# GELU feed-forward layer with its gradients: a smaller clear, b1 in two transfers, another bank for the first grad_out block, w2 evictions shared out, and gw1's half groups in a row at the end

## The chip, the cores and the metric

The kernel runs on one core of a Trainium2 chip. The metric is the time of one execution on the device in microseconds (us), where lower is better. Three runs of the kernel before gave a median of 285.6 us (285.5 to 286.16).

## The reference

The forward pass is a dense layer, a GELU in its tanh form and a second dense layer. The reference returns the output and the gradients of all five inputs:

```python
B, S, D, F = 1, 2048, 448, 1792        # everything in bf16
h = einsum("bsd,df->bsf", x, w1) + b1
h = gelu_tanh(h)
out = einsum("bsf,fd->bsd", h, w2) + b2
# and the vjp for grad_out:  gx, gw1, gb1, gw2, gb2
```

## The kernel before

D = 448 is three blocks of 128 and a rest of 64, so KD = 4 and the last block holds 64 rows only. The token axis is cut into 8 blocks of 256, the F axis into 7 pairs of 128-wide tiles. A step `n` is one pair in one block, 56 steps in all. The order of every instruction is written out by hand (`manual_schedule`), and each engine works through its own list in that order.

**Main loop, per step.** `M1` (L202) makes the pre-activation of two F tiles: 8 matmuls, four contraction blocks kt = 0 to 3 for each of the two tiles. The fourth block, kt = 3, uses `w1_sb[:, 3, :]`: its upper 64 partitions hold the rest of w1, its lower 64 are zero but for row 0, which holds b1. Row 0 of the fourth block of `xT_q` is one, so the bias comes in through the matmul. `M1` therefore needs the clear of that block, the load of w1's rest and the load of b1, at its fourth matmul. `M2` (L237) makes the output, `M4` (L224) grad_out times w2 transposed, `M6` (L255) gx, seven steps later. ScalarE (ACT) makes `hT` and the square `A`, then the tanh `Ct` and its square; VectorE (DVE) makes `Bt`, `A`, `Ep` and `ghT`; GpSimd (POOL) makes `Eq`. In block 0 there is no gx yet, and in its place TensorE turns w2 by transposes: `TR(c)` (L211) turns two tiles of w2 into a PSUM bank `psx`, and one copy (L214 on DVE or L216 on ACT) brings it into `w2T_sb`. There are seven such turns, before steps 0 to 6.

**Start.** GpSimd clears `warm` and the lower 64 partitions of `w1_sb[:, 3, :]` (L116). DVE builds the identity matrix `ident` in a chain of small instructions on `ramp` (L121) and `rowi` (L126). SP and ACT issue the loads: x of block 0 (`x_nat0`), w2 in four pieces, grad_out of block 0 (`g_nat0`), w1 in several column pieces (`load_w1`, rows of the first three blocks; `load_w1_last`, the rest), and b1 (L147) on ACT's queue behind the clear. b2 is loaded through GpSimd's queue (L157). TensorE turns x of block 0 (`turn_x0`, L175), runs `M1(0)`, `TR(0)`, turns grad_out of block 0 into a `psx` bank (`turn_g0`, L187), then `M1(1)`, `TR(1)`, `M2(0)`, `M4(0)`, `M1(2)`, `TR(2)` and so on. There are two `psx` banks, two `ps1`, two `ps4` and two output banks `pso0` and `pso1`; `M2` of a block accumulates in the output banks and `M2_out` (L243) empties them on DVE.

**End.** After the main loop come gw2 (L379) and gw1. For gw1 the F axis is cut into chunks of 256, 512, 512 and 512 columns. Each chunk has three full groups (L452: 16 matmuls with a 128x128 weight, evicted by ACT at L454 and stored by SP at L455) and then one half group, `half(ci)` (L432). A half group has 64 weight columns only, so the chunk's columns are split in two halves, and the two halves are computed side by side in the two column halves of the array (`tile_position=(0, h * DL)`): 32 matmuls. Each of the two results is evicted by itself and stored by itself (L443); for the last chunk ACT evicts the first half (L439) and DVE the second (L441).

Of the kernel before, what the change touches and what calls it, by code (L numbers as in the profile page):

```python
# [10 lines left out]
ALU = mybir.AluOpType  # L11
BF16 = mybir.dt.bfloat16
# [7 lines left out]
def kernel(  # L20
# [15 lines left out]
    nc = tc.nc  # L36
    P = 128
    B, S, D = x.shape
    F = w1.shape[1]
# [4 lines left out]
    KD = (D + P - 1) // P  # L44
    DL = D - (KD - 1) * P
# [5 lines left out]
    SPB = SB // P  # L51
# [13 lines left out]
    psop = ctx.enter_context(tc.tile_pool(name="psop", bufs=1, space=bass.MemoryType.PSUM))  # L65
    psxp = ctx.enter_context(tc.tile_pool(name="psxp", bufs=2, space=bass.MemoryType.PSUM))
# [20 lines left out]
    w1_sb = wts.tile([P, KD, F], BF16, name="w1_sb")  # L87
# [25 lines left out]
    ramp = wts.tile([P, P], F32, name="ramp")  # L113
    rowi = wts.tile([P, 32], F32, name="rowi")
    nc.gpsimd.memset(warm[:], 0.0)
    nc.gpsimd.memset(w1_sb[0:DL, KD - 1, :], 0.0)  # L116


    nc.vector.memset(ramp[:, 0:1], 0.0)
# [3 lines left out]
    for q in range(1, 4):  # L123
        nc.vector.tensor_scalar(out=rowi[32 * q:32 * q + 32, 0:1], in0=rowi[32 * q:32 * q + 32, 0:1],
                                scalar1=32.0 * q, scalar2=None, op0=ALU.add)
    nc.vector.tensor_scalar(out=ident[:], in0=ramp[:], scalar1=rowi[:, 0:1], scalar2=None, op0=ALU.is_equal)  # L126

    def load_w1(eng, f0, f1):
        eng.dma_start(out=w1_sb[:, 0:KD - 1, f0:f1],  # L129
                      in_=w1[0:(KD - 1) * P, f0:f1].rearrange("(k p) f -> p k f", p=P))  # L130

    def load_w1_last(eng, f0, f1):
        eng.dma_start(out=w1_sb[DL:P, KD - 1, f0:f1], in_=w1[(KD - 1) * P:D, f0:f1])
# [9 lines left out]
    nc.sync.dma_start(out=x_nat0[:], in_=x2[0:SB, :].rearrange("(j p) d -> p j d", p=P))  # L143
    load_w1(nc.scalar, 0, 256)
    load_w1_last(nc.scalar, 0, 512)
    nc.scalar.activation(out=warm_h[:], in_=warm[:, 0:64], func=ACT.Gelu_apprx_tanh)
    nc.scalar.dma_start(out=w1_sb[0:1, KD - 1, :], in_=b1.rearrange("(o f) -> o f", o=1))  # L147
    load_w2(nc.sync, 0, 2)
    nc.sync.dma_start(out=g_nat0[:], in_=g2[0:SB, :].rearrange("(j p) d -> p j d", p=P))  # L149
    load_w1(nc.sync, 256, 512)  # L150
    load_w2(nc.sync, 2, 4)
    load_w1(nc.sync, 512, 1024)
    load_w1_last(nc.sync, 512, F)
# [16 lines left out]
    def turn_x0(dst, src):  # L170
        for j in range(SPB):
            pt = psxp.tile([P, SPB, KD, P], BF16, name="psx")
            for kt in range(KD):
                lo = DOV if kt == KD - 1 else kt * P
                nc.tensor.transpose(pt[:, 0, kt, :], src[:, j, lo:lo + P], ident[:])  # L175
            if j == 0:
                nc.vector.tensor_copy(out=dst[:, :, j * P:(j + 1) * P], in_=pt[:, 0, :, :])
            else:
                nc.scalar.copy(out=dst[:, :, j * P:(j + 1) * P], in_=pt[:, 0, :, :])  # L179
        nc.vector.memset(dst[0:1, KD - 1, :], 1.0)  # L180

    def turn_g0(dst, src):
        pt = psxp.tile([P, SPB, KD, P], BF16, name="psx")
        for j in range(SPB):
            for kt in range(KD):
                lo = DOV if kt == KD - 1 else kt * P
                nc.tensor.transpose(pt[:, j, kt, :], src[:, j, lo:lo + P], ident[:])  # L187
        nc.scalar.copy(out=dst[:].rearrange("p k (j s) -> p j k s", j=SPB), in_=pt[:])
        nc.gpsimd.memset(dst[0:DL, KD - 1, :], 0.0)
# [16 lines left out]
    def TR(c):  # L206
        pt = psxp.tile([P, 2, KD, P], BF16, name="psx")
        for t in range(2):
            for kt in range(KD):
                lo = DOV if kt == KD - 1 else kt * P  # L210
                nc.tensor.transpose(pt[:, t, kt, :], w2_sb[:, 2 * c + t, lo:lo + P], ident[:])  # L211
        dst = w2T_sb[:, :, 2 * c * P:(2 * c + 2) * P].rearrange("p k (t f) -> p t k f", t=2)
        if c < 2:
            nc.vector.tensor_copy(out=dst, in_=pt[:])  # L214
        else:
            nc.scalar.copy(out=dst, in_=pt[:])  # L216
# [123 lines left out]
    for n in range(NSTEP):  # L340
        b, c = divmod(n, NP)
# [43 lines left out]

    with ExitStack() as wctx:
        wp = wctx.enter_context(tc.tile_pool(name="wp", bufs=1))
        gw1_all = wp.tile([P, KD, F], BF16, name="gw1_all")
        gw2_all = wp.tile([P, NF, D], BF16, name="gw2_all")
        x_all = wp.tile([P, NS, D], BF16, name="x_all")  # L390
        gsum = wp.tile([P, D], F32, name="gsum")
        gb2_w = wp.tile([P, D], BF16, name="gb2_w")
        gb1_all = wp.tile([P, F], BF16, name="gb1_all")
        gb1_row = wp.tile([1, F], BF16, name="gb1_row")
        out3_v = out_3.rearrange("(o f) -> o f", o=1)
        out4_v = out_4.rearrange("(ft p) d -> p ft d", p=P)

        chunks = [(0, 256), (256, 512), (768, 512), (1280, 512)]
        ghn = []
        for (f0, fw) in chunks:  # L400
            t = wp.tile([P, NS, fw], BF16, name=f"gh_nat{f0}")
            for k in range(fw // P):
                nc.sync.dma_start_transpose(out=t[:, :, k * P:(k + 1) * P], in_=ghT_dram[f0 + k * P:f0 + (k + 1) * P, :])
            ghn.append(t)
        nc.gpsimd.dma_start(out=x_all[:], in_=x2.rearrange("(st p) d -> p st d", p=P))

        nc.vector.tensor_reduce(out=gsum[:], in_=g_all[:].rearrange("p s d -> p d s"), axis=mybir.AxisListType.X, op=ALU.add)
        nc.gpsimd.partition_all_reduce(gb2_w[:], gsum[:], channels=P, reduce_op=bass_isa.ReduceOp.add)
        nc.gpsimd.dma_start(out=out_5.rearrange("(o d) -> o d", o=1), in_=gb2_w[0:1, :])

        for ft in range(NF):
            ps = early[ft] if ft < 2 else gw2_mm(ft)
            nc.scalar.copy(out=gw2_all[:, ft, :], in_=ps[:, 0:D])
            if ft in (4, 9, NF - 1):
                lo = {4: 0, 9: 5, NF - 1: 10}[ft]
                nc.sync.dma_start(out=out4_v[:, lo:ft + 1, :], in_=gw2_all[:, lo:ft + 1, :])

        for ci, (f0, fw) in enumerate(chunks):
            gacc = wp.tile([P, 512], F32, name="gacc", bufs=2)
            nc.vector.tensor_reduce(out=gacc[:, 0:fw], in_=ghn[ci][:].rearrange("p s f -> p f s"),  # L420
                                    axis=mybir.AxisListType.X, op=ALU.add)
            nc.gpsimd.partition_all_reduce(gb1_all[:, f0:f0 + fw], gacc[:, 0:fw], channels=P, reduce_op=bass_isa.ReduceOp.add)
        nc.gpsimd.tensor_scalar(out=gb1_row[:], in0=gb1_all[0:1, :], scalar1=0.5, scalar2=None, op0=ALU.mult)
        nc.gpsimd.dma_start(out=out3_v[0:1, :], in_=gb1_row[:])

        def half(ci):
            f0, fw = chunks[ci]
            hw = fw // 2
            ps = psxp.tile([P, 512], F32, name="psx")
            for s_ in range(NS):  # L430
                for h in range(2):
                    nc.tensor.matmul(ps[h * DL:(h + 1) * DL, 0:hw], lhsT=x_all[:, s_, (KD - 1) * P:D],  # L432
                                     rhs=ghn[ci][:, s_, h * hw:(h + 1) * hw],
                                     start=(s_ == 0), stop=(s_ == NS - 1), tile_position=(0, h * DL), skip_group_check=True)
            for h in range(2):
                src = ps[h * DL:(h + 1) * DL, 0:hw]
                dst = gw1_all[h * DL:(h + 1) * DL, KD - 1, f0 + h * hw:f0 + (h + 1) * hw]
                if h == 0 or ci + 1 < len(chunks):
                    nc.scalar.mul(out=dst, in_=src, mul=0.5)  # L439
                else:  # L440
                    nc.vector.tensor_scalar(out=dst, in0=src, scalar1=0.5, scalar2=None, op0=ALU.mult)  # L441
                eng = nc.scalar if h == 0 and ci + 1 == len(chunks) else nc.sync
                eng.dma_start(out=out_2[(KD - 1) * P:D, f0 + h * hw:f0 + (h + 1) * hw], in_=dst)  # L443

        i = 0
        for ci, (f0, fw) in enumerate(chunks):
            for kt in range(KD - 1):
                pool, name = (ps1p, "ps1") if i % 2 == 0 else (ps4p, "ps4")
                i += 1
                ps = pool.tile([P, 512], F32, name=name)  # L450
                for s_ in range(NS):
                    nc.tensor.matmul(ps[:, 0:fw], lhsT=x_all[:, s_, kt * P:(kt + 1) * P], rhs=ghn[ci][:, s_, :],  # L452
                                     start=(s_ == 0), stop=(s_ == NS - 1))
                nc.scalar.mul(out=gw1_all[:, kt, f0:f0 + fw], in_=ps[:, 0:fw], mul=0.5)  # L454
            nc.sync.dma_start(out=out_2[0:(KD - 1) * P, f0:f0 + fw].rearrange("(k p) f -> p k f", p=P),  # L455
                              in_=gw1_all[:, 0:KD - 1, f0:f0 + fw])
            half(ci)


# [28 lines left out]
```

## Time and profile before

| | |
|---|---|
| median of three runs | 285.6 us |
| the profiled execution | 285.71 us |
| its span, first to last instruction | 283.9 us |
| TensorE (PE) busy | 277.2 us, 98% |
| DVE, ACT, POOL busy | 78%, 55%, 33% |
| granted TensorE clock | 1.0 |

The profile comes from one execution. Busy time of TensorE is modelled at the end of each matmul, so two neighbouring matmuls overlap in the rows: the distance from start to start is what a matmul costs in a row of them. A row of the timeline names the start, the length, the engine, the line, the operation with its shapes, and in brackets how long the engine had been idle and what released it. A queue's name ends in q (SPq, ACTq). PEld is the loading of weights, which overlaps the matmuls.

### The profile page before, as it was taken

The page shows a single profiled execution, that of the slowest core. Times are in us where ns is not written, and L with a number is a line of the kernel's source. Part 1 is how long each engine was busy: PE and PEld are TensorE (multiplying, and loading weights), DVE is VectorE, ACT ScalarE, POOL GpSimd, SP SyncE. Part 2 cuts the span into 40 slices and gives each one's busy share as a digit, 9 for nine tenths or more (in the row PEclk, how much of TensorE's full clock was granted, in tenths as well). Part 3 has the DMA queues.
Part 4 walks back from the last instruction along what each step waited for, and adds up shares of the span by engine and source line. Part 5 has one row for each costly group of instructions (what it writes and reads, how often), then busy time and mean ns, then how long its engine had stood idle before and what let it go on. Part 6 is the DMA issues. An engine that isn't in the chain of part 4 may idle for free.

```text
span 283.9 us, 5012 instructions
## 1 busy us (share of the span) xinstructions
PE 277.2 (98%) x1969; PEld 182.7 (64%) x1969; DVE 221.1 (78%) x263; ACT 155.5 (55%) x282; POOL 94.3 (33%) x88
## 2 busy tenths in 40 slices
PE   7999999999999999999999999999999999999994
PEld 3787677777777777777777777765555557554542
DVE  5688988887888897798887888875976999999000
ACT  2799777667777667777677776752121121212211
POOL 4233343334255333433334423341052004040451
PEclk9999999999999999999999999999999999999999
DMA  7999874463558957539426453184999999501101
GB/s 201 334 147 228 165 154 123 124 117 88 164 132 257 236 149 121 134 109 148 124 85 146 102 151 98 34 196 106 327 181 208 208 181 266 168 27 38 62 5 65
DMA packets 108089, 41.96 MB, mean 148 GB/s; under 512 B 81089, under 2 KB 107137, under 8 KB 108066
## 3 DMA queue, kind: packets, MB, share of 16 engines
q1 hardware_dynamic: 106528, 37.56, 59.4%
q0 software_dynamic: 976, 3.79, 4.2%
q8 instruction: 15, 0.25, 0.4%
q10 hardware_dynamic: 562, 0.30, 0.4%
q14 instruction: 8, 0.07, 0.1%
HBM read 7.46 MB, written 14.23 MB: 76 GB/s over the span
## 4 chain that ended last, share of the span: by engine, by line
PE 94%; DMA 2%; DVE 1%; SPq 1%; ACT 1%; issue 0%; DVEq 0%
PE ps L224 17%; PE ps L202 16%; PE ps L379 15%; PE pso L237 15%; PE psx L255 15%; PE ps L452 13%; DMA w_sb<-in_w_dram 2%; PE psx L432 2%; PE psx L211 1%; DVE o_blk L243 0%; DVE Bt L282 0%; ACT hT L276 0%; ACT A L272 0%; SPq L129 0%; SPq L149 0%
## 5 line engine op out<-in xcount | busy, mean ns | idle before, releaser
L296 POOL TENSOR_TENSOR Eq<-Ct,Ep 128x512 bf16<-128x512 bf16 x56 | 64.7, 1156 | 112.9 <-DVE Ep L295 110.8
L282 DVE SCALAR_TENSOR_TENSOR Bt<-A,ps 128x512 f32<-128x512 f32 x56 | 38.4, 686 | 26.3 <-ACT A L272 26.3
L202 PE MATMUL ps<-xT_q,w_sb 128*128 128x256 bf16 x448 | 58.2, 273 | 0.4 <-ACT xT_q L179 0.2
L224 PE MATMUL ps<-gT_q,w2T_sb 128*128 128x256 bf16 x448 | 58.1, 273 | 0.1
L276 ACT ACTIVATE hT<-ps 128x512 bf16<-128x512 f32 x56 | 33.3, 595 | 44.6 <-PE ps L202 44.5
L420 DVE TENSOR_REDUCE gacc<-gh_nat 128x512 f32<-128x8192 bf16 (+1 forms) x4 | 49.7, 12460 | 4.7 <-DMA gh_nat<-ghT_dram 4.7
L224 PEld LDWEIGHTS <-w2T_sb 128*128 128x128 bf16 x448 | 43.7, 98 | 14.5 <-ACT Bt L289 0.5
L237 PE MATMUL pso<-w_sb,hT 128*128 128x448 bf16 x224 | 51.7, 352 | 0.4 <-DVE o_blk L243 0.4
L255 PE MATMUL psx<-w1T_sb,ghT 128*128 128x448 bf16 x224 | 50.5, 352 | 0.0
L202 PEld LDWEIGHTS <-w_sb 128*128 128x128 bf16 x448 | 43.7, 98 | 6.2 <-issue 0.9
L379 PE MATMUL ps<-g_all,h_nat 128*128 128x448 bf16 x224 | 42.5, 352 | 0.0
L283 DVE SCALAR_TENSOR_TENSOR A<-A,ps 128x512 f32<-128x512 f32 x56 | 38.5, 687 | 1.9
L301 DVE SCALAR_TENSOR_TENSOR ghT<-Eq,ps 128x512 bf16<-128x512 bf16 x56 | 38.2, 681 | 1.4 <-POOL Eq L296 1.3
L295 DVE SCALAR_TENSOR_TENSOR Ep<-Bt,A 128x512 bf16<-128x512 f32 x56 | 38.4, 685 | 0.4
L452 PE MATMUL ps<-gh_nat,x_all 128*128 128x512 bf16 (+1 forms) x192 | 37.0, 353 | 0.0
L289 ACT ACTIVATE Bt<-Ct 128x512 f32<-128x512 bf16 x56 | 35.3, 630 | 1.8
L288 ACT ACTIVATE Ct<-Bt 128x512 bf16<-128x512 f32 x56 | 35.6, 636 | 0.0
L379 PEld LDWEIGHTS <-h_nat 128*128 128x128 bf16 x224 | 21.9, 98 | 20.5
L237 PEld LDWEIGHTS <-hT 128*128 128x128 bf16 x224 | 21.7, 98 | 19.9 <-issue 0.9
L272 ACT ACTIVATE A<-ps 128x512 f32<-128x512 f32 x56 | 33.1, 592 | 0.0
L255 PEld LDWEIGHTS <-ghT 128*128 128x128 bf16 x224 | 21.9, 98 | 12.5
L452 PEld LDWEIGHTS <-x_all 128*128 128x128 bf16 x192 | 18.5, 98 | 17.5 <-issue 0.4
(47 smaller groups left out, 119.8 us busy)
## 6 DMA issues: line engine op xcount, KB each, us to landing
ghT_dram<-ghT SPq DMA_DIRECT2D x8, 512.0 KB, 3.0
ghT_dram<-ghT SPq DMA_DIRECT2D x8, 384.0 KB, 3.1
out_dram<-o_blk SPq DMA_DIRECT2D x8, 224.0 KB, 2.0
out_dram<-gx_blk SPq DMA_DIRECT2D x8, 224.0 KB, 2.1
g_all<-in_grad_out_dram POOLq DMA_DIRECT2D x1, 1792.0 KB, 9.6
x_all<-in_x_dram POOLq DMA_DIRECT2D x1, 1792.0 KB, 10.8
out_dram<-gw_all SPq DMA_DIRECT2D x3, 384.0 KB, 2.4
out_dram<-gw_all SPq DMA_DIRECT2D x2, 560.0 KB, 4.1
```

Of the source, the lines that this page charges most:

```text
L202: nc.tensor.matmul(ps1[:, t * SB:(t + 1) * SB], lhsT=w1_sb[:, kt, f], rhs=xq[:, kt, :], start=(kt == 0), stop=(kt == KD - 1))
L224: nc.tensor.matmul(ps4[:, t * SB:(t + 1) * SB], lhsT=w2T_sb[:, kt, (2 * c + t) * P:(2 * c + t + 1) * P], rhs=gq[:, kt, :], start=(kt == 0) ...
L237: nc.tensor.matmul(pso[j][:, 0:D], lhsT=hT[:, c, o:o + P], rhs=w2_sb[:, ft, :], start=(ft == 0), stop=(ft == NF - 1))
L255: nc.tensor.matmul(psx[:, 0:D], lhsT=ghT[:, ft // 2, o:o + P], rhs=w1T_sb[:, ft, :], start=(ft == 0), stop=(ft == NF - 1))
L282: nc.vector.scalar_tensor_tensor(out=Bt[:], in0=A[:], scalar=3.0 * GELU_C, in1=ps1[:], op0=ALU.add, op1=ALU.mult)
L283: nc.vector.scalar_tensor_tensor(out=A[:], in0=A[:], scalar=GELU_C, in1=ps1[:], op0=ALU.add, op1=ALU.mult)
L295: nc.vector.scalar_tensor_tensor(out=Ep[:], in0=s["Bt"][:], scalar=1.0, in1=s["A"][:], op0=ALU.subtract, op1=ALU.mult)
L296: nc.gpsimd.tensor_tensor(out=Eq[:], in0=s["Ct"][:], in1=Ep[:], op=ALU.subtract)
L301: nc.vector.scalar_tensor_tensor(out=blkt[b]["ghT"][:, c, :], in0=s["Eq"][:], scalar=1.0, in1=s["ps4"][:], op0=ALU.add, op1=ALU.mult)
L379: nc.tensor.matmul(ps[:, 0:D], lhsT=h_nat[:, bb * NP + c, t * SPB + sj, :], rhs=g_all[:, s_, :], start=(s_ == 0), stop=(s_ == NS - 1))
L420: nc.vector.tensor_reduce(out=gacc[:, 0:fw], in_=ghn[ci][:].rearrange("p s f -> p f s"), axis=mybir.AxisListType.X, op=ALU.add)
L452: nc.tensor.matmul(ps[:, 0:fw], lhsT=x_all[:, s_, kt * P:(kt + 1) * P], rhs=ghn[ci][:, s_, :], start=(s_ == 0), stop=(s_ == NS - 1))
```

## The change

GpSimd clears 512 of the 1792 columns of w1's fourth block; DVE clears the other 1280 after the turn of x. b1 comes in two transfers: 512 columns on ACT's queue, and 1280 columns on GpSimd's queue behind DVE's clear. The load of w1's columns 256 to 512 moves from SP's queue to ACT's, in front of b1. grad_out of block 0 is turned into the bank of `pso0`. The copies of w2's turns 3 and 5 move from ACT to DVE. In the end part all full groups of gw1 come first, and the half groups follow as chunks 1, 2, 3, 0; both halves of a half group are evicted by one ACT instruction into a small tile `low`, and all their stores go to SP, but for one of chunk 0, which goes to ACT.

```diff
-    nc.gpsimd.memset(w1_sb[0:DL, KD - 1, :], 0.0)
+    nc.gpsimd.memset(w1_sb[0:DL, KD - 1, 0:512], 0.0)
...
     load_w1(nc.scalar, 0, 256)
     load_w1_last(nc.scalar, 0, 512)
+    load_w1(nc.scalar, 256, 512)
     nc.scalar.activation(out=warm_h[:], in_=warm[:, 0:64], func=ACT.Gelu_apprx_tanh)
-    nc.scalar.dma_start(out=w1_sb[0:1, KD - 1, :], in_=b1.rearrange("(o f) -> o f", o=1))
+    b1_row = b1.rearrange("(o f) -> o f", o=1)
+    nc.scalar.dma_start(out=w1_sb[0:1, KD - 1, 0:512], in_=b1_row[:, 0:512])
     load_w2(nc.sync, 0, 2)
     nc.sync.dma_start(out=g_nat0[:], in_=g2[0:SB, :].rearrange("(j p) d -> p j d", p=P))
-    load_w1(nc.sync, 256, 512)
     load_w2(nc.sync, 2, 4)
...
         nc.vector.memset(dst[0:1, KD - 1, :], 1.0)
+        nc.vector.memset(w1_sb[0:DL, KD - 1, 512:F], 0.0)
+        nc.gpsimd.dma_start(out=w1_sb[0:1, KD - 1, 512:F], in_=b1_row[:, 512:F])
 
     def turn_g0(dst, src):
-        pt = psxp.tile([P, SPB, KD, P], BF16, name="psx")
+        pt = psop.tile([P, SPB, KD, P], BF16, name="pso0")
...
-        if c < 2:
+        if c in (0, 1, 3, 5):
             nc.vector.tensor_copy(out=dst, in_=pt[:])
         else:
             nc.scalar.copy(out=dst, in_=pt[:])
...
-        gw1_all = wp.tile([P, KD, F], BF16, name="gw1_all")
+        gw1_all = wp.tile([P, KD - 1, F], BF16, name="gw1_all")
...
+            low = wp.tile([P, 256], BF16, name="low", bufs=4)
+            nc.scalar.mul(out=low[:, 0:hw], in_=ps[:, 0:hw], mul=0.5)
             for h in range(2):
-                src = ps[h * DL:(h + 1) * DL, 0:hw]
-                dst = gw1_all[h * DL:(h + 1) * DL, KD - 1, f0 + h * hw:f0 + (h + 1) * hw]
-                if h == 0 or ci + 1 < len(chunks):
-                    nc.scalar.mul(out=dst, in_=src, mul=0.5)
-                else:
-                    nc.vector.tensor_scalar(out=dst, in0=src, scalar1=0.5, scalar2=None, op0=ALU.mult)
-                eng = nc.scalar if h == 0 and ci + 1 == len(chunks) else nc.sync
-                eng.dma_start(out=out_2[(KD - 1) * P:D, f0 + h * hw:f0 + (h + 1) * hw], in_=dst)
+                eng = nc.scalar if h == 0 and ci == 0 else nc.sync
+                eng.dma_start(out=out_2[(KD - 1) * P:D, f0 + h * hw:f0 + (h + 1) * hw], in_=low[h * DL:(h + 1) * DL, 0:hw])
...
             nc.sync.dma_start(out=out_2[0:(KD - 1) * P, f0:f0 + fw].rearrange("(k p) f -> p k f", p=P),
                               in_=gw1_all[:, 0:KD - 1, f0:f0 + fw])
-            half(ci)
+        for ci in (1, 2, 3, 0):
+            half(ci)
```

## The prediction, made before the change was run

> **What bounds the kernel now.** I read the page first: the span, the busy shares and the chain of work that ended last.
>
> ```profile
> span 283.9 us, 5012 instructions
> PE 277.2 (98%) x1969; PEld 182.7 (64%) x1969; DVE 221.1 (78%) x263; ACT 155.5 (55%) x282; POOL 94.3 (33%) x88
> PE 94%; DMA 2%; DVE 1%; SPq 1%; ACT 1%; issue 0%; DVEq 0%
> ```
>
> TensorE carries the chain for 94% of the span. So only four places can pay: the start before TensorE is fed, its stalls, what it loses between matmuls, and what follows its last matmul. The chain in order of time shows the start and the end:
>
> ```profile
> 2.76 6.88 DMA w_sb<-in_w_dram
> ...
> 236.74 5.24 PE ps L452 x48
> 241.98 1.01 PE psx L432 x32
> 243.00 10.47 PE ps L452 x48
> ...
> 278.13 1.89 PE psx L432 x32
> ```
>
> The first row is the load of w2 tiles 2 and 3, issued by SP at 2.76 and landed at 9.64. Next the timeline from 0 to 13 us, engine by engine, which shows what else was late:
>
> ```profile
> 1.19 1.62 POOL L116 MEMSET w_sb<- 64x1792 bf16 x1
> 6.50 0.46 PEld L202 LDWEIGHTS <-w_sb 128*128 128x128 bf16 x5 [0.22 <-issue]
> 8.28 1.05 PE L202 MATMUL ps<-xT_q,w_sb 128*128 128x256 bf16 x8 [0.15 <-DMA w_sb<-in_w_dram]
> 9.69 0.62 PE L211 MATMUL psx<-ident,w_sb 128*128 128x128 bf16 x8 [0.36 <-DMA w_sb<-in_w_dram]
> ```
>
> M1(1) and TR(1) wait for weights. Counted by starts the loss is larger than the bracketed idle time: with M1(0)'s fourth matmul at 6.53 and 0.109 us a matmul (0.056 a transpose), the five that are left take 0.55, TR(0) 0.45, turn_g0 0.45 and M1(1) 0.87, so TR(1) could start 2.32 us after that fourth matmul, at 8.85. It starts at 9.69: 0.84 us are lost. The fourth matmul itself came 0.13 us late, and its weights, not its moving data, were the last thing: they need b1, whose packet the DMA view, cut to 5.8 to 5.9 us, shows.
>
> Last, the timeline around one change from full to half groups and back, and the end:
>
> ```profile
> 252.65 0.81 PE L452 MATMUL ps<-gh_nat,x_all 128*128 128x512 bf16 x3
> 253.39 0.41 PE L432 MATMUL psx<-gh_nat,x_all 128*64 128x256 bf16 x4
> ...
> 254.73 0.60 PE L432 MATMUL psx<-gh_nat,x_all 128*64 128x256 bf16 x7
> 255.26 0.60 PE L452 MATMUL ps<-gh_nat,x_all 128*128 128x512 bf16 x2
> ...
> 280.04 0.38 ACT L439 ACTIVATE gw_all<-psx 64x256 bf16<-64x256 f32 x1 [1.27 <-PE psx L432]
> ...
> 280.44 0.43 DVE L441 TENSOR_SCALAR gw_all<-psx 64x256 bf16<-64x256 f32 x1 [17.98 <-ACT gw_all L439]
> 280.90 0.47 SPq L443 DMA_DIRECT2D out_dram<-gw_all  x1
> ```
>
> The third full matmul starts at 252.65 + 0.81 - 0.38 = 253.08, the half group at 253.39: 0.31 us, where full matmuls follow each other every 0.216. The last half matmul starts at 255.06, the next full one at 255.26: 0.20, where a pair of halves takes 0.109. Each way costs about 0.09, and the first matmuls behind each are 0.01 to 0.02 slow, so 0.11 a way. Groups of one kind show no such gap.
>
> **The end, by parts.** *Half groups in a row.* Now there are four ways in and three out, seven at 0.11. Afterwards there is one way in: 6 x 0.11 = 0.66 us of TensorE's own time, on the path. What one half group behind another costs is not in the trace. Its bounds are nothing (the nearest row: full group behind full group) and a full 0.11 each, which leaves 3 x 0.11 = 0.33. I take nothing, so **-0.66**. The chunks' transposes end early (SP issues the last by 238.2), so no group waits for data when it comes 1 to 5 us sooner. `gw1_all` shrinks, so the tiles behind it move over other main-loop tiles; the first of them is filled from 195.6 on and read from 236.7, which hides any wait there.
>
> *Behind the last matmul.* Now TensorE ends at 280.02 and the last store is issued at 280.90, 0.88 later: ACT 0.38, then DVE 0.43 in series. Afterwards one ACT eviction of 128 columns (0.27, the shortest of L439) lets both stores go 0.33 us after the last matmul. But SP still issues chunk 3's two stores, at 0.55 each from 0.44 behind that group, until 1.54. Chunk 0's half group ends some 0.84 behind it, so its store waits until 0.70 behind the last matmul. That saves 0.18, and a 128-column matmul ends 0.05 sooner behind its start: **-0.2**. If the two issues do not collide it is 0.55. POOL's last store (issued 277.82, landed 1.8 later) stays 2 us ahead of the end.
>
> **The start, by parts.** *The clear.* All uses of line 121:
>
> ```profile
> L121 DVE TENSOR_SCALAR ramp<-ramp x7: 153/182/1522, 0.9 to 3.5; 128x1 f32<-128x1 f32 x1, 128x2 f32<-128x2 f32 x1, 128x4 f32<-128x4 f32 x1, 128x8 f32<-128x8 f32 x1
> ```
>
> Of the seven (median 182 ns) one took 1522, and it ended as POOL's clear ended at 2.81. POOL's 512-column clear of `warm` took 0.52, so the new clear ends near 1.71 and ident (4.63) comes 1.1 us sooner. Then x is the limit: it lands at 4.03, so the turns start at 4.14, not 4.68, a gain of 0.54 that ends at M1(0)'s fourth matmul, which needs b1.
>
> *b1's first part.* It stands behind 192 KB more on ACT's queue, but is issued 0.4 us sooner. Low bound: 6.0, the old 6.5 less the earlier issue. High bound: w2 tiles 2 and 3 (224 KB) and b2 (112 KB, whose issue on POOL comes 1.1 us sooner) all go ahead of it, 336 KB at the 357 GB/s of 5 to 6 us, 0.95 us: 7.45. I take 6.9, nearer the high end since the 192 KB are on its own queue. TR(1) is then free at 9.22.
>
> *w1's columns 256 to 512 and w2's tiles 2 and 3.* SP issues the w2 piece one slot (0.51) sooner: 9.13 if its landing moves with the issue, 9.64 if the bytes decide. I take 9.3, so TR(1) starts 0.4 sooner. Bounds: 0.84 sooner (all in time), 0.1 later (b1 at 7.45). Later loads move up one slot too; if w2 tiles 4 to 7, landed at 12.47, did not, TR(2) (now 12.65) would cap the gain at 0.2. **-0.4**.
>
> The Trainium skill, "DMA: Bandwidth & Descriptors", section Issuing engines are not separate DMA queues, speaks against this move: all queues share the same 16 engines, and issuing from several saves only issue time. By it alone the start would give at most the 0.51 slot; the trace before cannot show the two orders side by side.
>
> *DVE's clear and b1's second part.* DVE's 256-column clear took 0.27; 1280 columns take 1.35, behind L180, so from 5.85 to 7.2 or from 6.39 to 7.75. The next DVE work, TR(0)'s copy, comes at 7.72, and its result is needed at 10.90, so even 1 us of delay is covered. POOL issues the second part near 7.5, before the patch of gT_q at 9.32, and the 0.7 us issue hides there. M1(2) needs it at its fourth matmul, 12.10, or 11.7 after the gain. POOL's queue shows these landings:
>
> ```profile
> b_bc<-in_b_dram POOLq DMA_DIRECT2D x1, 112.0 KB, 5.3
> out_dram<-gb_w POOLq DMA_DIRECT2D x1, 0.9 KB, 3.5
> out_dram<-gb_row POOLq DMA_DIRECT2D x1, 3.5 KB, 1.8
> ```
>
> The last ran with the DMA engines idle, the second under load like this one: 3.5, landed at 11.0, cost 0. The bounds are 1.8 (9.3) and 10.8 (x_all, 1.8 MB: 18.3).
>
> The same page of the Trainium skill, Anatomy of one DMA, gives such a transfer 2.0 us whatever its size; by that it would land at 9.5, and the sum would be the same.
>
> *The turn of grad_out in pso0.* M2(0) (10.14) now waits for the eviction, which ended at 9.26. With M1(0) 0.4 later and M2(0) 0.4 sooner, 0.1 us of cover is left; without it at most 0.3 of the start's gain is lost. Cost 0.
>
> **The w2 copies.** Two copies of 1.02 leave ACT and cost DVE 2 x 0.69 = 1.38. DVE had five waits of 0.28 for ACT's `A` between 17.0 and 29.3, 1.40 in all, because ACT was overfull (3.07 a step against TensorE's 2.95). With ACT lighter they go, and the copies fill them. TensorE's stalls near 28 to 33 us (M4 waiting for DVE's ghT, M2 for o_blk), about 1.1 us, hang on when DVE gets there, so they stay: **0**, between -0.1 and +0.6.
>
> **Sum.** 285.71 (span 283.9 and 1.8 around it) - 0.66 - 0.2 - 0.4 = 284.45; the median before, 285.6, is 0.1 below the profiled run, so **284.4**.
>
> **Rivals.** *The start gives nothing* (b1 as late as 7.4, or the bytes decide): -0.86, 284.8. For it: DMA engines are busy for 84% or more of each us from 3 on. Against: the two loads stood in one queue. Chance 0.22. *Each half group pays its own way in*: -0.93, 284.7. Nothing in the trace speaks for it. 0.1. *The whole 0.84 comes back*: -1.7, 284.0. For it: ident is ready 1.1 us sooner. 0.11. *Slower: b1's second part is late.* M1(2) stands until it lands; it decides from a landing 5.5 us after issue (13.0, which eats the 0.86 of the end as well). At x_all's 10.8 M1(2) starts its fourth matmul at 18.3, 6.2 later, less 0.86: 291. For it: the DMA engines are full from 8 to 14 us. Against: it is one row of 2.5 KB. 0.07. My forecast keeps 0.5.
>
> **How the numbers follow.** Without the slow rival and the farthest tenth the cases reach from 283.8 to 285.2. A difference of 0.3% (0.86 us) is about what a measurement of this kernel can tell from no change. Nearly all of the forecast (0.44), the large gain (0.11) and half of the first two rivals (0.16) lie beyond it: faster 0.71. Slower 0.06. Same 0.23.
>
> **What would show it.** Right: the L121 maximum falls below 0.6 us; TR(1) starts near 9.3; half groups follow each other without a gap; the last SP issue comes 0.7 behind the last matmul. Wrong: M1(2)'s fourth matmul waits for a DMA; M4 in block 0 waits longer for DVE; gaps of 0.1 between half groups.

## The result, and the profile after

The changed kernel takes 288.57 us (median of 6 executions, 286.73 to 290.01) where the kernel before takes 285.25 (284.87 to 286.16): a ratio of 1.0114, with a 95% interval of 1.0075 to 1.0153. The forecast was 284.4; it is slower by 1.1%. The profiled execution took 288.66 us. All times and ratios here are of executions in the same, fast state; one of b_w1b_act, at 292.14 us, fell in a slower state and is not counted.

From the page of the changed kernel: the span, the busy time, the granted TensorE clock in 40 slices of the span, and the shares of the chain that ended last.

```profile
span 286.9 us, 5010 instructions
PE 278.4 (97%) x1969; PEld 185.1 (65%) x1969; DVE 220.9 (77%) x265; ACT 153.2 (53%) x277; POOL 93.8 (33%) x89
PEclk9799999999999999999999999999999999999999
PE 96%; issue 1%; DVE 1%; ACT 0%; POOL 0%; DVEq 0%; POOLq 0%
```

TensorE still carries the chain. New is the 7 in the second slice of the clock row (7 to 14 us), and that TensorE is busy 1.2 us longer with as many matmuls. The chain in order of time, start, length and what it was:

```profile
7.01 2.87 issue
12.15 1.71 PE ps L205 x8
...
240.42 36.32 PE ps L451 x192
276.74 6.27 PE psx L435 x128
```

The first row is a hole of nearly 3 us in which the profile names nothing that TensorE waited for. The second is `M1(1)`: eight matmuls in 1.71 us, where 0.87 is usual. The last two are the end: 192 full and then 128 half matmuls without a break. The timeline of the first 14 us shows the hole (start, length, engine, what; in brackets the idle time before and its releaser):

```profile
1.83 0.61 ACTq L129 DMA_DIRECT2D w_sb<-in_w_dram  x1
...
3.27 0.29 DVE L126 TENSOR_SCALAR ident<-ramp,rowi 128x128 bf16<-128x128 f32 x1
4.26 1.06 PE L176 MATMUL psx<-ident,x_nat 128*128 128x128 bf16 x8
4.47 0.65 ACTq L149 DMA_DIRECT2D w_sb<-in_b_dram  x1
...
6.00 0.82 PE L205 MATMUL ps<-xT_q,w_sb 128*128 128x256 bf16 x3
6.41 0.59 DVE L182 MEMSET w_sb<- 64x640 uint32 x1
9.88 0.71 PE L205 MATMUL ps<-xT_q,w_sb 128*128 128x256 bf16 x5 [3.06 <-issue]
```

`M1(0)` runs its first three matmuls and stands 3.06 us before the fourth, the one that needs b1. b1's first part is issued by ACT at 4.47; before it was at 2.83. Then the windows: stretch, its length, PE busy with matmuls in brackets, the same for PEld, DVE, ACT and POOL, the granted clock, DMA share, GB/s.

```profile
9.80:10.60 0.80, 0.72 (x9) 0.69 (x10) 0.00 (x0) 0.00 (x0) 0.00 (x0) 1.00 1.06 336
10.60:13.50 2.90, 2.90 (x24) 2.44 (x22) 1.97 (x3) 2.10 (x3) 0.24 (x1) 0.50 1.05 351
```

0.7 us after TensorE is fed again, its clock falls to 0.50, and matmuls follow at 0.213 us where 0.109 is usual. By the clock's own records in the trace it stays at 0.50 for 3.4 us, from 10.61 to 14.02.

By the starts of matmuls the difference of the two traces is made of four pieces (gw2, between the second and the third, takes 42.37 us in both):

| piece (us) | before | after | difference |
|---|---|---|---|
| start of `M1(2)` | 11.77 | 15.91 | +4.14 |
| `M1(2)` to the first matmul of gw2 | 182.43 | 181.97 | -0.46 |
| first to last matmul of gw1 | 43.15 | 42.52 | -0.63 |
| start of the last matmul to the end of the span | 4.22 | 4.12 | -0.10 |
| sum, against spans of 283.95 and 286.90 | | | +2.95 |

So the end and block 0 gave 1.19 us, and the start took 4.14.

### The profile page after: what moved, and what is told of

Its sections match the earlier page's. It is cut to its first block, busy times and chain, and to the rows that moved or that the text cites. A ratio compares the mean times of both kernels' runs of the same rounds, so it can differ in the third digit from the quotient of the medians.

```text
span 286.9 us, 5010 instructions
## 1 busy us (share of the span) xinstructions
PE 278.4 (97%) x1969; PEld 185.1 (65%) x1969; DVE 220.9 (77%) x265; ACT 153.2 (53%) x277; POOL 93.8 (33%) x89
## 4 chain that ended last, share of the span: by engine, by line
PE 96%; issue 1%; DVE 1%; ACT 0%; POOL 0%; DVEq 0%; POOLq 0%
PE ps L205 17%; PE ps L227 17%; PE ps L382 15%; PE pso L240 15%; PE psx L258 14%; PE ps L451 13%; PE psx L435 2%; PE psx L214 1%; PE ps L169 1%; DVE o_blk L246 0%; PE psx L176 0%; PE pso L190 0%; DVE w_sb L182 0%; ACT xT_q L180 0%; POOL warm L115 0%
## 5 line engine op out<-in xcount | busy, mean ns | idle before, releaser
L205 PE MATMUL ps<-xT_q,w_sb 128*128 128x256 bf16 x448 | 59.4, 276 | 3.1 <-issue 3.1
```

The costliest lines, as they stand in the source:

```text
L205: nc.tensor.matmul(ps1[:, t * SB:(t + 1) * SB], lhsT=w1_sb[:, kt, f], rhs=xq[:, kt, :], start=(kt == 0), stop=(kt == KD - 1))
```

## The experiments

The theory: b1's first part is late, because it is issued late and because it stands on ACT's queue behind 192 KB of w1; the low clock follows from the hole. The rival: the DMA engines' bytes (b2, issued 1.1 us sooner, among them) make it late wherever it stands. "Fourth" below is the start of the fourth matmul of `M1(0)`, "block 0" the piece from `M1(2)` to gw2. Ratios are to the kernel before, with 95% intervals. Names that begin with a_ or best_ are edits of the kernel after, those with b_ of the kernel before.

**a_b1_first: b1 ahead of w1's columns on ACT's queue.**

```diff
-    load_w1(nc.scalar, 256, 512)
...
     nc.scalar.dma_start(out=w1_sb[0:1, KD - 1, 0:512], in_=b1_row[:, 0:512])
+    load_w1(nc.scalar, 256, 512)
```

> The changed kernel with b1's first part issued ahead of w1's columns 256 to 512 on ACT's queue. Theory Q (b1 is late because it stands behind that load on ACT's queue, issued at 4.47 where before it was 2.83, with 192 KB more ahead of it): b1 is issued near 1.8 to 2.4, M1(0)'s fourth matmul starts by 6.7 instead of 9.88, and the time falls by 2 us or more, to 286.5 or less; M1(1) may then wait for its columns. Theory B (b2's load, issued 1.07 us sooner on GpSimd's queue, holds the DMA engines while b1 is due): the fourth matmul still starts after 8.5 and the time stays within 1 us of 288.6.

289.16, 1.0115 [1.008, 1.0149]. b1 is issued at 1.90 and the fourth comes at 6.62, so b1's lateness is gone; the time is not. The timeline:

```profile
1.90 0.61 ACTq L148 DMA_DIRECT2D w_sb<-in_b_dram  x1
4.35 0.40 ACTq L129 DMA_DIRECT2D w_sb<-in_w_dram  x1
...
11.62 1.05 PE L205 MATMUL ps<-xT_q,w_sb 128*128 128x256 bf16 x8 [3.27 <-DMA w_sb<-in_w_dram]
```

Now w1's columns go out at 4.35, and `M1(1)` stands 3.27 us for them. Whichever of the two loads comes second on ACT's queue is issued near 4.4. The profiled execution took 287.34 us and kept its clock at 1.0; the other three, 288.69 to 289.92, have a mean clock of 0.994, as the kernel after has in its profile.

**a_w1b_on_sp: w1's columns back on SP's queue.**

```diff
-    load_w1(nc.scalar, 256, 512)
...
     nc.sync.dma_start(out=g_nat0[:], in_=g2[0:SB, :].rearrange("(j p) d -> p j d", p=P))
+    load_w1(nc.sync, 256, 512)
```

> The changed kernel with w1's columns 256 to 512 back on SP's queue in their old place. Theory Q: b1 is issued near 2.4, M1(0)'s fourth matmul starts by 6.7, M1(1) and TR(1) near 8.3 and 9.7 as before; the time is 284.6, the changed kernel's gain in the end part (0.7) and in block 0 (0.3) without its loss in the start. Theory B: the fourth matmul starts after 8.5, the time stays above 287.

285.49, 0.9997 [0.9984, 1.001], not the 284.6 that was expected. One line undone takes away the whole loss of time; the start is still late (`M1(2)` at 12.61, before at 11.77), and the end and block 0 make up for it. The fourth is at 6.24, but `M1(1)` still starts at 9.64 (8.28 before) and had waited 1.81 us for w1's columns on SP's old place. Something else makes these late.

**a_b2_late: b2's load, as the change has everything else, behind b1's second part on GpSimd's queue.**

```diff
-    nc.gpsimd.dma_start(out=b2_bc[:], in_=b2.rearrange("(o d) -> o d", o=1).to_broadcast((P, D)))
...
         nc.gpsimd.dma_start(out=w1_sb[0:1, KD - 1, 512:F], in_=b1_row[:, 512:F])
+        nc.gpsimd.dma_start(out=b2_bc[:], in_=b2.rearrange("(o d) -> o d", o=1).to_broadcast((P, D)))
```

> The changed kernel with b2's load behind b1's second part on GpSimd's queue, so issued near 7.8 instead of 1.68. Theory Q: b1 is still issued near 4.5 behind the 192 KB, M1(0)'s fourth matmul starts after 8, the time stays above 287. Theory B: it starts by 7, the time falls to 286 or less.

288.32, 1.0104 [1.0073, 1.0134]. The fourth comes at 8.66, 1.22 sooner, and the clock falls there too, so little is won. b2 in the way is a part, not the whole.

**a_sp_b2late: the last two edits together.**

> The changed kernel with both repairs: w1's columns 256 to 512 back on SP's queue, and b2's load behind b1's second part on GpSimd's queue. If the start's loss is the sum of the two (b1's first part late, and b2's early load slowing the loads it meets), M1(1) starts by 8.0 and M1(2) by 11.2, where the kernel before has 8.28 and 11.77, and the time is 284.0, faster than before by over 0.4%. If b2 does not matter, M1(2) stays near 12.6 and the time at 285.5.

285.23, 0.9982 [0.9968, 0.9997]. `M1(1)` starts at 7.77: b2, not DVE's or ACT's queue, had held w1's columns up in a_w1b_on_sp. But now this waits:

```profile
7.26 0.64 POOL L182 DMA_DIRECT2D w_sb<-in_b_dram  x1 [5.53 <-DVE w_sb L181]
...
10.74 0.49 PE L205 MATMUL ps<-xT_q,w_sb 128*128 128x256 bf16 x3
12.92 0.72 PE L205 MATMUL ps<-xT_q,w_sb 128*128 128x256 bf16 x5 [1.69 <-DMA w_sb<-in_b_dram]
```

This is `M1(2)`, which needs b1's second part. It was issued at 7.26 and landed 5.6 us later: the mechanism of the prediction's slower rival. It costs 1.86 us, as block 0 takes 183.83 against 181.97.

**b_b2_late: before, b2's load alone moved behind the patch of `gT_q`.**

> The kernel before with b2's load behind the patch of gT_q on GpSimd's queue, issued near 9.6 instead of 2.75; nothing else is changed. If b2's packets are what made M1(1) and TR(1) wait (8.28 and 9.69), M1(1) starts near 8.0 and TR(1) near 8.9, M1(2) 0.8 sooner (11.0), and the time is 284.7. If they waited for bytes alone, M1(2) stays within 0.2 of 11.77 and the time within 0.3 of before.

285.0, 0.9975 [0.9965, 0.9986]. `M1(1)` at 8.11, `TR(1)` at 8.98, `M1(2)` at 11.06, 0.71 sooner than before. Most of the loss of 0.84 us at the start, which the prediction read from the trace of before, was made by b2's 112 KB. One trace would not carry this, since five traces with the start of before have `M1(2)` between 11.20 and 11.93; the ratio of the times does, as 0.25% are 0.7 us.

**a_slot_free: after, w2's first two pieces as one load.**

```diff
-    load_w2(nc.sync, 0, 2)
+    load_w2(nc.sync, 0, 4)
...
-    load_w2(nc.sync, 2, 4)
```

> The changed kernel with w2's tiles 0 to 3 in one load, so that b1's first part is one of the first eight loads on the hardware queues and no longer waits for an earlier load's landing; it stays behind w1's columns 256 to 512 on ACT's queue. Theory wait (the 4.47 issue is what made b1 late): b1 is issued near 2.5 and M1(0)'s fourth matmul starts by 7.5. Theory place (192 KB ahead on its queue are what made it late): b1 is issued near 2.5 and the fourth matmul still starts after 8.5. Either way M1(1) and TR(1) may move as well, since w2's tiles 0 and 1 land with 2 and 3.

286.77, 1.0055 [1.0025, 1.0085]. The timeline:

```profile
1.84 0.61 ACTq L129 DMA_DIRECT2D w_sb<-in_w_dram  x1
2.55 0.52 ACTq L149 DMA_DIRECT2D w_sb<-in_b_dram  x1
8.38 0.95 PE L204 MATMUL ps<-xT_q,w_sb 128*128 128x256 bf16 x5 [1.89 <-DMA w_sb<-in_b_dram]
```

With one load less ahead of it b1 is issued at 2.55, not 4.47, directly behind w1's columns. In each of these kernels the first eight loads of SP and ACT together raise eight different semaphores and go out without a wait. The ninth raises the first one's again, and the program has it wait until that load, w1's columns 0 to 256, has landed, at about 4.4; in the kernel after the ninth is b1. Here the profile also names what the hole waits for: b1. The fourth comes 1.50 sooner than in the kernel after: that is the price of being the ninth. The other 1.76, to the 6.62 of a_b1_first, come with standing behind w1's columns; 0.65 of them are the later issue (2.55 against 1.90), and b2's bytes are in them, too.

**a_warm14: after, with 14 instead of 2 dummy matmuls (128x512) of `warm` ahead of `M1(0)`.**

> The changed kernel with 14 instead of 2 matmuls on the cleared tile between the turn of x and M1(0): TensorE has work until about 9 while b1 is due. It leaves every load as it is. In the changed kernel the granted clock was 0.5 from 10.6 to 13.5 us. If that costs 1.6 (five steps' matmuls at twice their distance), the fourth matmul still starts near 9.9, the distances from there are 0.109, M1(2) starts near 14.3 instead of 15.91 and the time falls by 1.6 to 287.0. If the low clock has nothing to do with the wait, no change.

287.35, 1.0075 [1.0042, 1.0108]. The timeline of TensorE and the clock:

```profile
5.12 3.82 PE L169 MATMUL ps<-warm 128*128 128x512 bf16 x14
8.78 0.49 PE L205 MATMUL ps<-xT_q,w_sb 128*128 128x256 bf16 x3
10.21 0.71 PE L205 MATMUL ps<-xT_q,w_sb 128*128 128x256 bf16 x5 [0.93 <-issue]
```

The clock stays at 1.00 (9.8 to 14.6 us). From the fourth to `M1(2)` it takes 4.41 us, in the kernel after 15.91 - 9.88 = 6.03: the low clock costs 1.62. The six executions of the kernel after show the same price: 286.73 us with a mean clock of 0.998, 288.35 to 288.66 with 0.993 or 0.994, 289.37 and 290.01 with 0.988 and 0.987 (3.4 us at half rate take 0.006 off the mean). So the median of 288.57 holds one such fall, and the one execution without it is still 1.5 us slower than before. The dummies do not rule the fall out: two of nine executions here have 0.994 and 0.993 and took 290.08 and 290.45.

**b_w1b_act: before, with the one line moved that takes w1's columns to ACT.**

> The kernel before with one line moved: w1's columns 256 to 512 on ACT's queue ahead of b1. By theory Q this one move makes most of the loss: b1 is issued near 4.4 instead of 2.83, M1(0)'s fourth matmul starts between 8.4 and 9.9 instead of 6.53, and the time is 287.5 to 289. If it needs the early b2 as well, the fourth matmul starts by 7.5 and the time is below 286.5.

286.81, 289.9 and 290.13, 1.0102 [1.005, 1.0154]. b1 is issued at 4.66, the fourth comes at 8.93, `M1(2)` at 16.17. One line makes the loss; a_w1b_on_sp takes it away again.

**b_end_only: before, with the whole change of the end part** (half groups 1, 2, 3, 0 behind all full ones, `low`, the stores).

> The kernel before with the end part alone changed (half groups in a row at the end, one eviction, small tile). From the two traces: TensorE's time from the first full group to the last half group falls from 43.28 to 42.6, and what follows the last matmul stays at 3.9, so 0.7 less: 284.6 against 285.25. If the drain also falls as predicted it is 0.9 less. A rival, that the half groups' stores now crowd SP's queue and give the gain back: no change.

285.31, 0.999 [0.9976, 1.0004]. gw1 takes 42.52 from first to last matmul (43.15), and 4.09 us follow the last one's start (4.22): 0.76 in the profile. In the median hardly anything of that arrives. Traces of kernels with the same start differ by as much: `M1(2)` comes at 11.93 here, at 11.77 before and at 11.44 in b_tr_only.

**b_tr_only: before, with the copies of turns 3 and 5 on DVE.**

```diff
-        if c < 2:
+        if c in (0, 1, 3, 5):
```

> The kernel before with the copies of turns 3 and 5 on DVE, nothing else. The prediction: 0, DVE fills its waits with the copies and the stalls near 28 to 33 us stay. The two traces: from M1(2) to M4(7) the kernel before takes 20.65 (11.77 to 32.42), the changed one 20.32 (15.91 to 36.23), so 0.33 less: 285.2, too little for the timing to show but visible in those starts.

286.03, 1.0006 [0.999, 1.0023]. Block 0 falls from 182.43 to 181.98, as it does in the kernel after, but this too is less than a comparison of medians resolves.

**b_b2late_end_tr: before, with b2 late, the new end and the two copies.**

> The kernel before with b2's load late, the end part changed and turns 3 and 5 on DVE; the start's clear, b1 and the order of the loads stay as before. Sum of the parts by their profiles: 0.7 for b2, 0.6 for the end, 0.3 for the turns, 284.1. If the parts hide each other, 284.8.

285.19, 0.9976 [0.9957, 0.9994], not the sum of its parts (284.1). Block 0 and gw1 have their 181.97 and 42.52, but 5.0 us follow the start of the last matmul, not 4.2; the next run shows why.

**best_dve_clear: after, with w1's columns on SP, b2 late, and b1 in one transfer again; DVE clears its 1280 columns as its very first instruction.**

```diff
+    nc.vector.memset(w1_sb[0:DL, KD - 1, 512:F], 0.0)
...
-    load_w1(nc.scalar, 256, 512)
...
-    nc.scalar.dma_start(out=w1_sb[0:1, KD - 1, 0:512], in_=b1_row[:, 0:512])
+    nc.scalar.dma_start(out=w1_sb[0:1, KD - 1, :], in_=b1_row)
```

> The changed kernel with both repairs and without b1's second part: DVE clears w1's 1280 columns as its first instruction (0.59 us in the changed kernel's profile), GpSimd the other 512, b1 comes in one transfer on ACT's queue, b2's load behind the patch of gT_q. In the run with both repairs M1(2) started at 10.74 and its fourth matmul then stood 1.96 for b1's second part. If that wait was the last loss of the start, ident comes near 4.2, M1(1) near 7.8, M1(2) near 10.8 and TR(2) near 11.7, and the time is 283.4, 0.8% under before. The other possibility is that w1's later columns or w2's tiles 4 to 7 land no sooner than 12.4: then TR(2) stands and the time is 284.2.

284.93, 0.9954 [0.9934, 0.9973]. `M1(2)` starts at 11.04, block 0 and gw1 take 181.97 and 42.52, and gw1's last matmul starts 1.82 us sooner than before. But 5.3 us follow its start, not 4.1. The chain that ended last no longer goes through TensorE:

```profile
264.10 3.23 POOL gb_all L424
267.33 0.07 POOLq L425 x2
267.41 7.65 issue
275.06 4.76 POOL gb_row L425
279.82 0.27 issue
280.09 0.74 POOLq L482
```

It ends with gb1: DVE's reductions, GpSimd's sums over partitions (`gb_all`), 7.65 us without work, the scaling by 0.5 (`gb_row`), the store at 280.1. The last gw1 store goes out at 278.47.

**best_gb1_dve, b_b2l_end_tr_gb1 and b_gb1_dve: the scaling of gb1 on DVE,** in best_dve_clear, in b_b2late_end_tr and in the kernel before.

```diff
-        nc.gpsimd.tensor_scalar(out=gb1_row[:], in0=gb1_all[0:1, :], scalar1=0.5, scalar2=None, op0=ALU.mult)
+        nc.vector.tensor_scalar(out=gb1_row[:], in0=gb1_all[0:1, :], scalar1=0.5, scalar2=None, op0=ALU.mult)
```

> best_dve_clear with one word changed: the scaling of gb1 by 0.5 (1x1792) on DVE, not on POOL. Theory (POOL's gb1 chain ends last there): in best_dve_clear POOL stands 7.65 us between its last sum over partitions (ended 267.33) and this scaling, which takes 4.76, and its store is issued at 280.12, 1.65 behind the last gw1 store (278.47); with DVE, free from 264.0 on, the store goes near 270, the span behind the last matmul's start falls from 5.30 to about 4.1, and the time from 284.9 to about 283.8. Rival (what lies behind the last matmul there is the gw1 stores' own landing, slowed by something else): 5.3 stays, 284.9.

> The kernel before with four things: b2's load behind the first block's work on GpSimd's queue, the half groups in a row with their new eviction, the copies of w2's turns 3 and 5 on DVE, and the scaling of gb1 on DVE (the first three alone took 285.19, with 5.02 us behind the start of the last matmul). Theory (POOL's gb1 chain ends last): 4.1 us behind the last matmul's start, and the time falls by 0.9 to 284.3. Rival (the stores themselves land late): 5.0 stays, 285.2.

> The kernel before with one word changed: the scaling of gb1 by 0.5 on DVE, not on POOL. Both theories: before POOL's last store is issued at 277.82, 3.08 ahead of the last gw1 store at 280.90, so nothing comes of it: 285.6, ratio 1.000, and 4.2 us behind the start of the last matmul. If it gains too, POOL's chain ended last there as well, against the profile of before. If it loses, DVE's use of gb1's row delays the evictions of the last gw1 groups.

289.69 (1.0143 [1.0118, 1.0168]), 290.33 (1.0158 [1.0137, 1.0179]) and 289.51 (1.0122 [1.0099, 1.0144]). The theory was right on the end (4.0, 4.0 and 4.2 us behind the start of the last matmul) and the expected time was missed all three times, the control included. One instruction at the end costs 4 us, and they are lost in block 0: in the control it takes 186.70, not 182.43, and `M4(2)` starts at 19.19, before at 16.80. Some 1.7 of the 4 us are again the clock, which falls to 0.50 at 19.24: the one execution of six with a mean clock of 1.0 took 287.73, the others 289.25 to 289.62. GpSimd's waits in b_gb1_dve (waiting instruction, releaser, sum, times, longest):

```profile
POOL Eq L296 <- DVE Ep L295: 104.8, 53, 3.3
POOL gb_w L408 <- DVE gsum L407: 11.1, 1, 11.1
POOL Eq L296 <- issue: 7.3, 1, 7.3
```

The first `Eq` of the program, at 17.18 (13.04 before), stood 7.3 us with nothing to wait for. The wait of 7 us ahead of `gb_row` has moved from the end of one execution to the start of the next. The packed trace, though not the timeline, has an instruction at this place: a pair of MODIFY_POOL_CONFIG at 9.87, ahead of `Eq`. Before, the pair ahead of `gb_row` is at 265.74 and 7.0 us pass behind it; a pair also stands ahead of `Eq`, at 9.83, but `Eq` starts as soon as DVE's `Ep` is there. So it seems that the program sets GpSimd up anew for another kind of work, and that this takes time only when it was set up for the other kind; this is read from names and places in the trace and not tested.

**best_gb1_tail and b_gb1_tail: the same, with one small operation on GpSimd behind the store of gb1.**

```diff
+        last = wp.tile([1, 8], BF16, name="last")
+        nc.gpsimd.tensor_scalar(out=last[:], in0=gb1_all[0:1, 0:8], scalar1=0.5, scalar2=None, op0=ALU.mult)
```

> best_gb1_dve with one instruction more on GpSimd: behind the store of gb1 it scales 1x8 values of gb1's sums into a scratch tile that nothing reads. What was seen: with gb1's scaling on DVE, GpSimd's last computation of the program is a sum over partitions, and its first tensor operation of the next execution (Eq, at 18.34 in the profile) stood 8.3 us with nothing to wait for; with the scaling on GpSimd 7.0 to 7.7 us stood ahead of that scaling, at the end, and none ahead of Eq. Theory (GpSimd pays about 7 us when it changes from the sum over partitions to a plain operation, in the next execution if need be): here the 7 us stand ahead of the small operation, near 277 at most, Eq waits for DVE alone, the start of gw2 comes back to 193.0, some 4 us lie behind the last matmul's start, and the time is 283.7. Rival (the move of the scaling to DVE delays Eq in another way): Eq still stands 8 us, 289.7.

> The kernel before with gb1's scaling on DVE, as in b_gb1_dve (289.5 against 285.5), and the same small operation on GpSimd behind the store of gb1. Theory (7 us at the change from the sum over partitions to a plain operation, paid wherever that comes next): the stall ahead of the first Eq goes, 7 us stand ahead of the small operation, and the time is that of the kernel before, 285.5. Rival (the move of the scaling itself delays Eq): 289.5.

283.64 (282.95 to 283.9), 0.9926 [0.9908, 0.9943], and 285.22, 0.9997 [0.9981, 1.0012]: as the theory put them. The end of best_gb1_tail on GpSimd and ACT's queue:

```profile
265.18 3.23 POOL L424 PARTITION_ALL_REDUCE gb_all<-gacc  x1 [10.87 <-DVE gacc L422]
269.36 0.51 POOL L426 DMA_DIRECT2D out_dram<-gb_row  x1 [0.94 <-DVE gb_row L425]
277.37 0.27 POOL L428 TENSOR_SCALAR last<-gb_all 1x8 bf16<-1x8 bf16 x1 [7.51 <-issue]
...
278.49 0.53 ACTq L443 DMA_DIRECT2D out_dram<-low  x1
```

The 7.5 us stand ahead of an operation that nothing needs, and the store of gb1 is issued at 269.36. This kernel is 0.7% faster than the one before and 1.7% faster than the change. Its span is 1.9 us shorter than before: 0.71 from the start, 0.46 from block 0, 0.63 from gw1, 0.13 behind the last matmul.

## Why the prediction was wrong

*b1's first part* is the step that failed. The prediction put it at 6.9 with 7.45 as its upper bound; the fourth matmul came at 9.88. Two things were left out. The issue was taken as 0.4 us sooner; it was 1.64 later, since b1 had become the ninth load (1.50 of the loss, a_slot_free). The trace of before had shown the sign: SP ended its fifth issue at 3.25 and issued its next load, w1's columns 512 to 1024, only at 4.44. The view of SP's own waits from 0 to 10 us says for what, the landing of other columns of w1, which this load does not need:

```profile
SPq L129 <- DMA w_sb<-in_w_dram: 1.2, 1, 1.2
```

And the bound for the bytes let 336 KB pass at the best rate of the trace, 0.95 us, as if all queues shared evenly; behind w1's columns on one queue b1 came 1.76 later than ahead of them (a_slot_free against a_b1_first, 0.65 of it the issue), and b2, counted only as bytes in that sum, cost 1.22 (a_b2_late; these prices overlap and do not add).

The second part of the loss was in no case of the prediction: a hole in TensorE's work that costs clock. Of the +4.14 at `M1(2)`, 3.35 are the hole (the fourth matmul at 9.88, not 6.53), 1.62 the clock (a_warm14), and -0.83 the old waits of `M1(1)` and `TR(1)`, which have gone only because everything came later. None of the prediction's three signs of being wrong appears in the trace; one of its signs of being right fails, `TR(1)`, which starts at 13.66 and not near 9.3.

*w1's columns 256 to 512 and w2's tiles 2 and 3*, -0.4: the opposite sign (b_w1b_act). The 0.84 us were there to be had, but b2 stood in the way, not the order of SP's loads: b_b2_late gets about 0.7 of it by moving b2. The Trainium skill's rule in "DMA: Bandwidth & Descriptors", section Issuing engines are not separate DMA queues, which the prediction weighed against the move, points the right way: the second issuing engine gave nothing here. It says nothing of the loss that the move brought.

*The clear* was right in its mechanism: the longest instruction of L121 fell from 1522 to 451 ns, the row from the answer for that line being

```profile
L121 DVE TENSOR_SCALAR ramp<-ramp x7: 154/181/451, 0.9 to 2.4; 128x1 f32<-128x1 f32 x1, 128x2 f32<-128x2 f32 x1, 128x4 f32<-128x4 f32 x1, 128x8 f32<-128x8 f32 x1
```

and x's turns started at 4.26 (4.14 predicted). It is worth nothing while b1 is late.

*DVE's clear and b1's second part*: the clear took 0.59 us, not 1.35: its row has 640 words of 32 bits, 0.92 ns each, where the 256 elements behind the estimate took 1.05 ns each. The landing was mis-sized: 5.6 us, not 3.5. The kernel after hides it (`M1(2)`'s fourth matmul is at 16.24), and a_sp_b2late shows the slower rival's mechanism at its point of decision, 5.5. The Trainium skill, "DMA: Bandwidth & Descriptors", section Anatomy of one DMA, gives a fixed cost of about 2.0 us to such a transfer; under this load that is far off. So the rival that ended slower had a real mechanism, but not the one that decided; its 0.07 and the total of 0.06 for slower were too low for a change that moves loads about in the one stage where the DMA engines are full.

*The turn of grad_out in pso0*: 0, as predicted. *The w2 copies*: 0 predicted, -0.46 in the traces (b_tr_only, and the piece in the kernel after); the time of b_tr_only does not resolve it. Of TensorE's stalls near 28 to 33 us, some 1.1 us that were to stay, this part went; that it went with ACT's surplus work was not tested by itself.

*Half groups in a row*: -0.66 predicted, -0.63 measured. *Behind the last matmul*: -0.2 predicted, -0.10 measured (-0.13 in b_end_only). The stores still collide on SP; of the profile after:

```profile
282.14 0.38 ACT L439 ACTIVATE low<-psx 128x256 bf16<-128x256 f32 x1 [1.36 <-PE psx L435]
283.04 0.28 ACT L439 ACTIVATE low<-psx 128x128 bf16<-128x128 f32 x1 [0.51 <-PE psx L435]
283.34 0.52 ACTq L442 DMA_DIRECT2D out_dram<-low  x1
```

SP's two stores of chunk 3 go from 282.5 on, at some 0.55 each, and its last only at 283.8, 0.8 behind TensorE's end at 282.99. And the cover of GpSimd's chain was read as 2 us: with TensorE's work all in time it is less than nothing (best_dve_clear).

Why the clock fell in some holes and not in others is taken up in the last section. What stays open is why the transposed loads of `gh_nat` came later in best_dve_clear (DVE's first sum for gb1 at 211.8, before at 210.1), though TensorE was 1.2 us ahead.

## What to carry to other kernels

Before a load is moved to another engine's queue, count the loads that are under way and look for an issue that waits for the landing of a load it does not need: that is the sign that the program's semaphores for loads are all in use, and that the next load will be held back, too. Where the DMA engines are full, judge a load by what stands ahead of it on its queue, not by the bytes of all queues at their best rate; and ask what a load off the path (here b2) does to those on it. When the bound engine gets faster, follow the other chains to their ends again, and when an operation is moved off an engine, ask what that engine will do next, even in the next execution.

## What the runs showed of the hardware that was not expected

GpSimd stands about 7 us without work when an operation such as `Eq` or the scaling of gb1 follows a sum over partitions: 6.8 to 7.7 us ahead of `gb_row` in the fourteen kernels that scale gb1 on GpSimd, before and after among them. Without that operation it stands 7.3 to 8.3 us ahead of the next execution's first `Eq`, and with an operation of 0.27 us at the end 6.8 to 7.5 us ahead of that. Clears (MEMSET) in between run without this wait, as the one at 9.54 in b_gb1_dve.

TensorE's clock fell to 0.50 behind holes of 1.89 us (a_slot_free), 2.04 (b_gb1_dve) and 3.06 (after), and not behind one of 3.27 (a_b1_first, in the profiled execution); one fall cost 1.62 us. In every trace the clock's records, but for the last, last a whole number of steps of 3.41 us. In all nineteen traces together the clock fell after 26 steps at full clock, those behind the last matmul included, and TensorE was busy for at most 1.53 us in each. After the other steps it stayed, and TensorE was busy for 1.72 us or more in each but for two, with 1.48 (a_b1_first) and 1.52 (a_sp_b2late). So in these traces the work within a step of 3.41 us decides, with a limit near 1.5 us, and not the length of a hole. The hole of 3.27 lies across two steps, which have 1.48 and 2.08 us of work; the whole hole of 1.89 lies in one, which has 1.33. The Trainium skill, "TensorE: Matmul & The Clock Gate", Part 1, gives half rate after an idle window of about 3.4 us that runs freely. The steps of 3.41 us agree with that; the seven falls at a hole do not, as TensorE was busy for 0.60 to 1.53 us in each of their steps.

Eight loads on the queues of SP and ACT go out at once and the ninth waits for the first one's landing: 1.5 us at this kernel's start. The wait is one of the compiled program, whose ninth load shares a semaphore with the first; what the queues would take without it, no run shows.
